# Adding the causal mask on VectorE while it takes the maximum, and turning one more pair with VectorE's block transpose

## The chip, the cores and the metric

The kernel runs on one core of a Trainium2 chip. The metric is the device time of one execution in microseconds (us), given as the median of the runs. A change of about 0.5% (4.4 us here) is what can be told from no change.

## The reference

Three layers follow each other, for a batch of 4 sequences of 448 positions with 768 channels. All data are 32-bit floats.

```python
q_n, k_n = rmsnorm(q, g_q), rmsnorm(k, g_k)          # (4, 12 heads, 448, 64)
x = softmax(q_n @ k_n.T / 8) @ v                     # attention; heads side by side: (4, 448, 768)
u = x + token_mlp(x)                                 # relu MLP along the 448 positions, 256 hidden
y = u + relu(u @ w_ch1) @ w_ch2                      # MLP along the channels, 1536 hidden
# four experts, each a single causal head of width 64; the two best by gate are mixed
for e in range(4):
    s = (y @ wq[e]) @ (y @ wk[e]).T / 8
    s = where(causal, -1e9, s)                       # position i sees positions up to i
    a = softmax(s)                                   # s - max, exp, divide by the sum
    out += gate[:, :, e] * (a @ (y @ wv[e]) @ wo[e])
```

## The kernel before

**Pairs.** Heads are worked on two at a time. A sequence has 6 plain pairs of the first attention, named (b, pr) with pr from 0 to 5, and 2 causal pairs (four experts). The 448 positions lie in 4 chunks of 112 partitions (`CP`). Each pair goes through `stack` (loads q and k, scales k), `score` and `finish` (the product with v).

**Scores and softmax** (`weighted`). For a chunk c, TensorE writes the scores of both heads into one PSUM tile, 112 partitions by 2 heads by w columns (L596). w is 448 for a plain pair and 112 times (c + 1) for a causal one. Two chunks make one step of TensorE work. For a causal pair the step ends with one more matmul per chunk and head (L601): the identity `eye` times `veil`, a 112x112 tile that holds -1e9 above its diagonal, is accumulated into the last 112 columns. VectorE then takes the negated maxima of both heads in one `tensor_reduce` (`top`, L566) into `nm`, and ScalarE computes exp(score + nm) with the row sum as a second output, one instruction per head (L581).

**Transposing the weights.** The product with v needs the softmax weights transposed, and there are two ways. `flip` does it with TensorE transposes of 112-column blocks into PSUM (L626 for plain pairs, 28 of them for a pair; L650 for causal pairs), and copies out of PSUM by ScalarE or VectorE (L431, L432). `turn` does it with VectorE: 4 transposes by 32x32 blocks (L700), and then 16 copies between groups of 32 partitions (quarters) that put the blocks in their places (L712), on VectorE, ScalarE or GpSimd. With `turn` the scores lie on 128 partitions, the positions of q are read in another order (arranged on the host in `_layout`), and the row of softmax sums reaches DRAM by one DMA instead of four (`spread`). A pair that uses it is called wide. Before the change all plain pairs of the third and fourth batch are wide (`b >= LATE`, LATE = 2), 12 pairs in all.

**What else runs.** `channel` is the MLP along the channels, by far the largest part of TensorE's work; its products (`mm3`, L520) are three matmuls on a split of each number into two parts. In the first batch the weights are also unpacked and split, by ScalarE, VectorE and GpSimd (L465 to L472, `split`), and kept in DRAM for the later batches. `project` makes the experts' q, k and v, and `combine` the output.

**The order of work.** Nothing is ordered by hand. Every step is entered with `add`, with its engine or engines and an estimated cost, and `Plan` lays out all steps of all four batches with a list schedule by priority, ten rounds, of which the one with the shortest estimated span is used. Each engine then runs its instructions in that order. A changed cost or a changed step can therefore move other steps too. The plain pairs of batch b + 1 are entered together with the causal pairs of batch b - 1, around `channel(b)`, so that attention and MLP can be laid beside each other. Tiles come from rings of buffers (`RING`): score, transposed and weight tiles of all pairs share the tag "s" with 3 buffers, and there are 2 PSUM tiles of scores. `flip` takes 2 buffers of "s" for a pair, `turn` 3.

`Stats` computes the inverse norms of q and k for a group of pairs (`root`, L835 to L846, a Newton iteration on VectorE or a power on GpSimd, by the planner's costs).

Of the kernel before, what the change touches and what calls it, by code (L numbers as in the profile page):

```python
# [9 lines left out]
F32 = mybir.dt.float32  # L10
F32R = mybir.dt.float32r
# [3 lines left out]
ALU = mybir.AluOpType  # L15
# [4 lines left out]
MASKED = -1e9  # L20
# [21 lines left out]

FAST = {(0, 0), (0, 1)}

LATE = 2


class Buf:
# [268 lines left out]
def kernel(  # L317
# [15 lines left out]
    nc = tc.nc  # L333
# [3 lines left out]
    P, CP, NCH, D = 128, 112, 4, 64  # L337
    S = CP * NCH
# [53 lines left out]
    def rows_ns(n):  # L392
        return 1.652 * n

    def flip_ns(n):
# [4 lines left out]

    ident = cp.tile([P, P], F32, tag="ident", name="ident")
    make_identity(nc, ident)
    dark = cp.tile([CP, CP], F32, tag="dark", name="dark")
    nc.gpsimd.memset(dark, 0.0)
    nc.gpsimd.affine_select(
        dark, dark, [[-1, CP]], ALU.is_ge, MASKED, base=0, channel_multiplier=1)
    veil = cp.tile([CP, CP], F32R, tag="veil", name="veil")
    nc.vector.tensor_copy(veil, dark)
    eye = cp.tile([CP, CP], F32R, tag="eye", name="eye")
    nc.vector.tensor_copy(eye, ident[:CP, :CP])  # L410
    ggs = cp.tile([P, 2], F32, tag="ggs", name="ggs")
    nc.scalar.dma_start(ggs, gg)
    half = cp.tile([CP, 1], F32, tag="half", name="half")
# [138 lines left out]
    def weighted(st, causal, sm, col, rq, alone, wide=False):  # L552

        q, k = st
        R = P if wide else CP  # L560
        s = sbuf([R, NCH, 2, S], F32, "s")
        nm = sbuf([P, NCH, 2], F32, "nm")

        def top(c, pst, w):
            dve(2 * w, [pst], [(nm, c)],
                lambda e: e.tensor_reduce(  # L566
                    nm.t[:R, c], pst.t[:R, :, :w], axis=AX.X, op=ALU.max, negate=True))

        def scale(cs):
            at = slice(cs[0], cs[-1] + 1)  # L570
            add({"DVE": (130, True), "POOL": (200, True)}, 0, [rq[0]], [(nm, c) for c in cs],
                lambda e: ENG[e].tensor_tensor(  # L572
                    nm.t[:R, at], nm.t[:R, at], rq[1]()[:, :, at].rearrange("p j c -> p c j"),
                    op=ALU.mult))

        def exps(c, pst, w):
            for j in range(2):
                add("ACT", act_ns(w, True, 2 if rq is None else 3),
                    [pst, (nm, c), *([rq[0]] if rq else [])],
                    [(s, (j, c)), (sm, 4 * (col + j) + c)],  # L580
                    lambda j=j: nc.scalar.activation(  # L581
                        s.t[:, c, j, :w], pst.t[:R, j, :w], AF.Exp,
                        bias=nm.t[:R, c, j : j + 1],
                        scale=1.0 if rq is None else rq[1]()[:, j, c : c + 1],
                        accum_out=sm.t[:, col + j, c : c + 1]))

        width = [CP * (c + 1) if causal else S for c in range(NCH)]
        for cs in [(c,) for c in range(NCH)] if alone else [(0, 1), (2, 3)]:
            ps = {c: pss() for c in cs}

            def mms(ps=ps):
                for c, pst in ps.items():
                    w = width[c]
                    for j in range(2):
                        me = slice(64 * j, 64 * j + 64)
                        nc.tensor.matmul(  # L596
                            pst.t[:R, j, :w], q.t[me, CP * c : CP * c + R], k.t[me, :w],
                            start=True, stop=not causal)
                for c, pst in ps.items() if causal else ():
                    for j in range(2):  # L600
                        nc.tensor.matmul(  # L601
                            pst.t[:CP, j, width[c] - CP : width[c]], eye, veil,
                            start=False, stop=True)

            add("PE", sum(rows_ns(width[c]) + (290 if causal else 0) for c in cs),
                [q, k], list(ps.values()), mms, mode="rows")
            for c, pst in ps.items():
                top(c, pst, width[c])
            if rq is not None:
                scale(cs)  # L610
            for c, pst in ps.items():
                exps(c, pst, width[c])
        return s
# [234 lines left out]
    class Stats:  # L848


        def __init__(self, b, qs, ks):
            n, m = len(qs), len(ks)
            self.qs, self.ks = qs, ks
            R = self.R = P if b >= LATE else CP
            st = self.st = sbuf([R, 3, 64], F32, "st")
            x, y, z = (lambda k=k: st.t[:CP, k, : 8 * (n + m)] for k in range(3))
            if R > CP:
                add("POOL", pool_ns(64), [], [st], lambda: nc.gpsimd.memset(st.t[96:, 1], 1.0))
            at = lambda t, pr: 8 * (ks.index(pr) + n if t else qs.index(pr))
            self.at = at  # L860
            for pr in sorted({*qs, *ks}):
                if (b, pr) in FAST:
                    for t in (1, 0):
                        if pr not in (qs, ks)[t]:
                            continue
                        q, part, qv = natural(b, pr, t)
                        sq = pss()
                        o = at(t, pr)
                        add("ACT", act_ns(512, True), [(q, part)], [sq],
                            lambda sq=sq, qv=qv, t=t: nc.scalar.activation(  # L870
                                sq.t[:CP, 0], qv()[:, t].rearrange("p g d -> p (g d)"), AF.Square))
                        dve(512, [sq], [(st, o)], lambda e, sq=sq, o=o: e.tensor_reduce(
                            x()[:, o : o + 8], sq.t[:CP, 0].rearrange("p (g d) -> p g d", d=D),
                            axis=AX.X, op=ALU.add))
                    continue
                q, part, qv = natural(b, pr, 0)
                i = qs.index(pr)
                x0 = lambda i=i: x().rearrange("p (t i g) -> p t i g", t=2, i=n)[:, :, i]
                add({"ACT": (act_ns(1024), False), "POOL": (pool_ns(1024), True)}, 0, [], [(q, part)],
                    lambda e, qv=qv: nc.scalar.activation(qv(), qv(), AF.Square) if e == "ACT"  # L880
                    else nc.gpsimd.tensor_mul(qv(), qv(), qv()))
                add({"DVE": (dve_ns(1024), False),
                     "POOL": (sum(pool_ns(16 << k) for k in range(6)), True)}, 0,
                    [], [(q, part), (st, i)], lambda e, x0=x0, qv=qv: fold(e, x0(), qv()))
            add({"DVE": (11 * (150 + 8 * (n + m)), True), "POOL": (400 + 1330 * (n + m), True)},
                0, [], [st], lambda e: root(e, x(), y(), z()))
            if (b, ks[0]) in FAST:

                q, part, qv = natural(b, ks[0], 1)
                kd = self.kd = sbuf([CP, NCH, 2, D], F32, "xn")  # L890
                o = at(1, ks[0])
                dve(512, [st, (q, part)], [kd], lambda e: e.tensor_tensor(
                    kd.t.rearrange("p c j d -> p j c d"),
                    qv()[:, 1].rearrange("p (j c) d -> p j c d", j=2),
                    y()[:, o : o + 8].rearrange("p (j c) -> p j c", j=2).unsqueeze(3)
                    .to_broadcast([CP, 2, NCH, D]),
                    op=ALU.mult), port=True)
                return
            rs = self.rs = plan.buf(dr, [2 * m, S], F32, f"rs_{b}_{ks[0]}")
            load(20, [st], [rs], lambda: nc.sync.dma_start(  # L900
                rs.t.rearrange("g (p c) -> p g c", c=NCH),
                y()[:, 8 * n :].rearrange("p (g c) -> p g c", c=NCH)))

        def q(self, pr):
            o = self.at(0, pr)
            return self.st, lambda: self.st.t[: self.R, 1, o : o + 8].rearrange(
                "p (j c) -> p j c", j=2)

        def k(self, pr):
# [21 lines left out]
    class Pair:  # L931
# [10 lines left out]
        def stack(self):  # L942
# [1 line left out]
                self.st = ex[self.b][2][self.pr]  # L944
                return
            b, pr = self.b, self.pr
            wide = self.wide = b >= LATE
            v = self.v = sbuf([P, NCH, 2, D], F32, "v")
            q, k = sbuf([P, S + 16], F32, "q"), sbuf([P, S], F32, "k")
            load(237, [], [q], lambda: nc.sync.dma_start(q.t, qkt[b, pr, 0]))  # L950
# [277 lines left out]
def _layout(i):  # L1228
# [7 lines left out]
    for at in FAST:  # L1236
        kn[at] = chunks(x[:, 1])[at]
    qn = chunks(x[:, 0]).copy()
    qn[LATE:] = rows(x[:, 0])[LATE:]
    nat = np.stack([qn, kn], axis=3).reshape(b, h // 2, s // 4, 2, 2 * 4, d)  # L1240
    ends = [(0, 512 - s), (0, 0)]
    v = np.pad(x[:, 2], [(0, 0)] * 3 + ends)
    v[:, :, 1] = np.pad(x[:, 2, :, 1], [(0, 0)] * 2 + [ends[0][::-1], (0, 0)])
    vals = v.reshape(b, h // 2, 2, 4, 128, d).transpose(0, 1, 4, 3, 2, 5)
    qkt = x[:, :2].transpose(0, 2, 1, 3, 5, 4).reshape(b, h // 2, 2, 2 * d, s).copy()
    late = qkt[LATE:, :, 0]
    qkt[LATE:, :, 0] = (
        late.reshape(*late.shape[:-1], s // 4, 4).swapaxes(-1, -2).reshape(late.shape))
    qkt = np.pad(qkt, [(0, 0)] * 4 + [(0, 16)])
    g = np.stack([i["g_q"], i["g_k"]], axis=1)  # L1250
    gg = np.concatenate([g, g], axis=0)
# [54 lines left out]
```

## Time and profile before

| what | us |
|---|---|
| median of 3 runs (875.44 to 878.80) | 878.48 |
| the profiled execution, its own time | 877.03 |
| its span in the trace | 875.2 |
| TensorE (PE) busy in the span | 834.5 |
| VectorE (DVE) busy | 609.2 |
| ScalarE (ACT) busy | 460.9 |
| GpSimd (POOL) busy | 122.0 |

The profiled execution is 1.45 us below the median, and 1.8 us of its time lie outside the span of the trace. Busy time of TensorE is modelled: its matmuls overlap, so the mean of one matmul is longer than the distance from one to the next. Where the text needs the price of matmuls it takes the distance between starts.

### The profile page before, as it was taken

Reading aid. Unit: us, or ns where it says so; the run is one execution under the profiler, and the core shown is the slowest. Engines: PE = TensorE matmul, PEld = TensorE weight load, DVE = VectorE, ACT = ScalarE, POOL = GpSimd, SP = SyncE. Lnnn points to the kernel's source line nnn. Section 1 sums busy time; section 2 is a strip of 40 time slices with the busy share of each in tenths; the row PEclk is TensorE's granted clock in tenths of the full one; section 3 lists DMA queues with packets and bytes.
Section 4 is the critical chain, followed back from the end, with each engine's and each line's share of the span. In section 5 each row is a group of like instructions: output and inputs, shape, how many; then the busy total and the mean of one; then the engine's idle time right before and its main releaser. Section 6 shows DMA issues by size and latency. Waiting matters only on the chain.

```text
span 875.2 us, 13600 instructions
## 1 busy us (share of the span) xinstructions
PE 834.5 (95%) x4656; PEld 645.1 (74%) x4656; DVE 609.2 (70%) x1254; ACT 460.9 (53%) x1075; POOL 122.0 (14%) x154
## 2 busy tenths in 40 slices
PE   2899899999999999999999999999999999999998
PEld 1345478777768886887676786887776799998886
DVE  6988889899997568637699677846588671224342
ACT  5798756677665447324376655513286630002443
POOL 3234310011031011010131100100131100001000
PEclk9999999999999999999999999999999999999999
DMA  7656568888778926797655724696555316676334
GB/s 221 164 166 216 166 184 274 278 268 289 255 222 266 309 76 204 203 271 241 169 170 140 208 70 124 185 279 183 177 159 155 107 53 187 219 237 203 105 132 163
DMA packets 109749, 168.41 MB, mean 192 GB/s; under 512 B 17936, under 2 KB 76432, under 8 KB 109680
## 3 DMA queue, kind: packets, MB, share of 16 engines
q1 hardware_dynamic: 109536, 167.54, 63.5%
q8 instruction: 37, 0.61, 0.3%
q14 instruction: 32, 0.26, 0.1%
q10 hardware_dynamic: 144, 0.00, 0.0%
HBM read 136.66 MB, written 30.84 MB: 191 GB/s over the span
## 4 chain that ended last, share of the span: by engine, by line
PE 73%; DVE 15%; ACT 5%; DMA 4%; issue 2%; SPq 0%; DVEq 0%; ACTq 0%
PE a L520 50%; PE s L596 8%; PE m L725 8%; DVE nm L566 3%; ACT s L581 3%; PE m L751 2%; PE s L650 2%; DVE s L712 2%; DMA whl<-kept_c 2%; PE s L626 2%; DVE wraw L470 1%; DMA nat<-in_nat_dram 1%; DVE wraw L472 1%; PE s L601 1%; DVE s L700 1%
## 5 line engine op out<-in xcount | busy, mean ns | idle before, releaser
L520 PE MATMUL a<-uhl,whl 128*128 128x448 f32 x1152 | 244.4, 367 | 4.4 <-DVE hid L1097 2.6
L520 PEld LDWEIGHTS a<-uhl,whl 128*128 128x128 f32 x1152 | 214.0, 189 | 33.4 <-issue 8.7
L520 PE MATMUL a<-hid,whl 128*128 128x448 f32 x864 | 184.9, 367 | 2.5 <-DVE u L1108 1.6
L520 PEld LDWEIGHTS a<-hid,whl 128*128 128x128 f32 x864 | 159.4, 188 | 28.8 <-issue 9.3
L581 ACT ACTIVATE s<-s,nm,st 112x448 f32<-112x448 f32 (+1 forms) x192 | 137.1, 724 | 82.4 <-POOL nm L572 28.6
L566 DVE TENSOR_REDUCE nm<-s 112x2 f32<-112x896 f32 (+4 forms) x128 | 123.8, 996 | 35.8 <-PE s L601 18.7
L596 PE MATMUL s<-k,q 64*112 64x448 f32 (+4 forms) x512 | 113.2, 555 | 9.6 <-ACT s L581 8.0
L436 ACT ACTIVATE hid<-a 128x448 fp32r<-128x448 f32 x41 | 22.3, 544 | 134.1 <-PE a L520 134.0
L725 PE MATMUL m<-s,v 128*64 128x448 f32 x384 | 77.5, 546 | 0.0
L596 PEld LDWEIGHTS s<-k,q 64*112 64x112 f32 (+1 forms) x512 | 41.1, 184 | 49.2 <-issue 24.0
L1108 DVE TENSOR_TENSOR u<-a,u 128x448 f32<-128x448 f32 x72 | 44.7, 621 | 44.1 <-PE a L520 43.3
L1097 DVE SCALAR_TENSOR_TENSOR hid<-a,hid 128x448 fp32r<-128x448 f32 x48 | 29.7, 620 | 60.2 <-ACT hid L436 60.0
L712 ACT COPY s<-s 32x896 f32<-32x896 f32 (+1 forms) x74 | 61.9, 837 | 6.2 <-DVE s L700 3.9
L712 DVE COPY s<-s 32x896 f32<-32x896 f32 (+1 forms) x88 | 59.6, 677 | 1.5
L700 DVE STREAM_TRANSPOSE s<-s 128x896 f32<-128x896 f32 x48 | 51.3, 1094 | 12.3 <-ACT s L581 10.8
L450 POOL TENSOR_TENSOR uhl<-u,uhl 128x448 fp32r<-128x448 f32 x22 | 25.9, 1180 | 218.8 <-PE a L520 116.0
L725 PEld LDWEIGHTS m<-s,v 128*64 128x64 f32 x384 | 25.4, 136 | 41.5 <-issue 40.0
L431 ACT ACTIVATE s<-s 112x448 f32<-112x448 f32 (+5 forms) x76 | 36.3, 528 | 19.2 <-PE s L650 15.2
L581 ACT ACTIVATE s<-s,nm 112x112 f32<-112x112 f32 (+3 forms) x64 | 30.8, 494 | 25.8 <-DVE nm L566 25.6
L465 ACT ACTIVATE wraw<-w 128x256 f32<-128x256 f32 (+3 forms) x72 | 33.3, 465 | 13.5 <-DMA w<-in_wc_dram 11.3
L520 PE MATMUL a<-whl,uhl 128*112 128x260 f32 x288 | 39.1, 288 | 0.0
L581 ACT ACTIVATION_READ_ACCUMULATOR s<-s,nm,st 112x1 f32 (+1 forms) x192 | 38.9, 203 | 0.0
(146 smaller groups left out, 1047.2 us busy)
## 6 DMA issues: line engine op xcount, KB each, us to landing
whl<-kept_c SPq DMA_DIRECT2D x72, 384.0 KB
whl<-kept_c SPq DMA_DIRECT2D x108, 256.0 KB
w<-in_wc_dram SPq DMA_DIRECT2D x24, 384.0 KB
kept_c<-whl SPq DMA_DIRECT2D x24, 384.0 KB
w<-in_wc_dram SPq DMA_DIRECT2D x36, 256.0 KB
kept_c<-whl SPq DMA_DIRECT2D x36, 256.0 KB
whl<-kept_qk SPq DMA_DIRECT2D x24, 384.0 KB
nat<-in_nat_dram SPq DMA_DIRECT2D x19, 448.0 KB
```

Of the source, the lines that this page charges most:

```text
L431: lambda e: nc.scalar.activation(dst(), src(), AF.Copy) if e == "ACT"
L450: either(n, reads, writes, lambda e: e.tensor_tensor(dst()[:, 1], src(), f(dst()[:, 0]), op=ALU.subtract))
L465: add("ACT", act_ns(n), [(d, 1)], [(r, part)], lambda: nc.scalar.activation(rf(), half(1).bitcast(F32), AF.Copy, scale=2.0 ** -112))
L520: nc.tensor.matmul(acc, lhs[:, x], rhs[:, y], start=first and i == 0, stop=last and i == 2)
L566: lambda e: e.tensor_reduce(nm.t[:R, c], pst.t[:R, :, :w], axis=AX.X, op=ALU.max, negate=True))
L581: lambda j=j: nc.scalar.activation(s.t[:, c, j, :w], pst.t[:R, j, :w], AF.Exp, bias=nm.t[:R, c, j : j + 1], scale=1.0 if rq is None else r ...
L596: nc.tensor.matmul(pst.t[:R, j, :w], q.t[me, CP * c : CP * c + R], k.t[me, :w], start=True, stop=not causal)
L700: dve(2 * S + 64, [(s, (j, r)) for j in range(2)], [(t, r)], lambda e, r=r: e.transpose(t.t[:, :, 32 * r : 32 * r + 32], s.t[:, r].rearran ...
L712: lambda e, a=a, o=o, w=w, at=at: (nc.scalar.copy if e == "ACT" else ENG[e].tensor_copy)(at(p.t[32 * o : 32 * o + 32, :, P * a : P * a + N ...
L725: nc.tensor.matmul(av.t[64 * j : 64 * j + 64, q0:S], vat(j, c)[1](), p.t[:, j, c, q0:] if causal else p.t[:, 3 * j + c], start=c == 0, sto ...
L1097: lambda e, hl=hl, pa=pa: e.scalar_tensor_tensor(hl.t[:, 1], pa.t[:, :S], 0.0, f(hl.t[:, 0]), op0=ALU.max, op1=ALU.subtract))
L1108: dve(S, [pa], [u], lambda e, u=u, pa=pa: e.tensor_add(u.t, pa.t[:, :S], u.t))
```

## The change

The mask is no longer accumulated by TensorE. `veil` becomes a 112x448 tile of zeros with the mask in its last 112 columns, and for a causal pair VectorE runs one `tensor_tensor_reduce` per chunk and head (`veiled`): it adds `veil` to the scores, multiplies by -1, writes that back to PSUM over the scores, and leaves the minimum, which is the negated maximum, in `nm`. ScalarE then takes exp with a scale of -1. The tiles `dark` and `eye` go.

`LATE` becomes a pair, (1, 5): the last plain pair of the second batch is wide too, so `turn` takes the place of `flip` for it. The group of inverse norms that holds it lies on 128 partitions. The planner's cost of `root` on VectorE rises from 150 to 192 ns an instruction.

```diff
-LATE = 2
+LATE = (1, 5)
...
-    dark = cp.tile([CP, CP], F32, tag="dark", name="dark")
-    nc.gpsimd.memset(dark, 0.0)
+    veil = cp.tile([CP, S], F32, tag="veil", name="veil")
+    nc.gpsimd.memset(veil, 0.0)
     nc.gpsimd.affine_select(
-        dark, dark, [[-1, CP]], ALU.is_ge, MASKED, base=0, channel_multiplier=1)
-    veil = cp.tile([CP, CP], F32R, tag="veil", name="veil")
-    nc.vector.tensor_copy(veil, dark)
-    eye = cp.tile([CP, CP], F32R, tag="eye", name="eye")
-    nc.vector.tensor_copy(eye, ident[:CP, :CP])
+        veil[:, S - CP :], veil[:, S - CP :], [[-1, CP]], ALU.is_ge, MASKED, base=0,
+        channel_multiplier=1)
...
+        def veiled(c, pst, w):
+            for j in range(2):
+                dve(w, [], [pst, (nm, (c, j))], lambda e, j=j: e.tensor_tensor_reduce(
+                    pst.t[:CP, j, :w], pst.t[:CP, j, :w], veil[:, S - w :], -1.0, 3e38,
+                    op0=ALU.add, op1=ALU.min, accum_out=nm.t[:CP, c, j : j + 1]))
...
-                    [pst, (nm, c), *([rq[0]] if rq else [])],
+                    [pst, (nm, (c, j) if causal else c), *([rq[0]] if rq else [])],
...
-                        scale=1.0 if rq is None else rq[1]()[:, j, c : c + 1],
+                        scale=-1.0 if rq is None else rq[1]()[:, j, c : c + 1],
...
-                            start=True, stop=not causal)
-                for c, pst in ps.items() if causal else ():
-                    for j in range(2):
-                        nc.tensor.matmul(
-                            pst.t[:CP, j, width[c] - CP : width[c]], eye, veil,
-                            start=False, stop=True)
-
-            add("PE", sum(rows_ns(width[c]) + (290 if causal else 0) for c in cs),
+                            start=True, stop=True)
+            add("PE", sum(rows_ns(width[c]) for c in cs),
                 [q, k], list(ps.values()), mms, mode="rows")
             for c, pst in ps.items():
-                top(c, pst, width[c])
+                (veiled if causal else top)(c, pst, width[c])
...
-            R = self.R = P if b >= LATE else CP
+            R = P if (b, max(qs + ks)) >= LATE else CP
...
-            add({"DVE": (11 * (150 + 8 * (n + m)), True), "POOL": (400 + 1330 * (n + m), True)},
+            add({"DVE": (11 * (192 + 8 * (n + m)), True), "POOL": (400 + 1330 * (n + m), True)},
...
-            wide = self.wide = b >= LATE
+            wide = self.wide = (b, pr) >= LATE
```

The other edits follow from these two: `Stats.q` and the host's `_layout` ask for the pair (b, pr) instead of the batch.

## Rows read from the trace of the kernel before

**Rows 1.** The page's first part: busy us, share of the span, instructions.

```profile
PE 834.5 (95%) x4656; PEld 645.1 (74%) x4656; DVE 609.2 (70%) x1254; ACT 460.9 (53%) x1075; POOL 122.0 (14%) x154
```

**Rows 2.** Busy time by stretch: PE, PEld, DVE, ACT, POOL, PEclk, DMA share, GB/s.

```profile
240.00:270.00 30.00, 29.55 (x159) 20.04 (x155) 29.28 (x58) 18.81 (x46) 11.39 (x10) 1.00 0.76 245
270.00:300.00 30.00, 30.00 (x212) 25.10 (x211) 17.02 (x45) 15.52 (x44) 1.20 (x2) 1.00 0.90 269
300.00:330.00 30.00, 30.00 (x224) 24.62 (x223) 20.46 (x65) 14.47 (x43) 2.75 (x3) 1.00 0.37 130
330.00:360.00 30.00, 27.32 (x122) 20.85 (x121) 27.21 (x44) 21.35 (x42) 4.23 (x5) 0.94 0.71 215
...
420.00:450.00 30.00, 30.00 (x149) 20.91 (x147) 22.45 (x35) 15.91 (x34) 4.86 (x6) 1.00 0.53 150
...
840.00:860.00 20.00, 20.00 (x151) 16.63 (x151) 10.63 (x48) 9.24 (x25) 0.00 (x0) 1.00 0.40 141
```

**Rows 3.** The mask's matmuls: a step on TensorE's timeline (start, us).

```profile
276.97 0.60 PE L601 MATMUL s<-veil,eye 112*112 112x112 f32 x4
277.41 2.64 PE L520 MATMUL a<-uhl,whl 128*128 128x448 f32 x12
```

**Rows 4.** All instructions of line 601: ns min/median/max, first and last start.

```profile
L601 PE MATMUL s<-veil,eye x64: 260/262/308, 277.0 to 841.9; 112*112 112x112 f32 x64
```

**Rows 5.** Timeline of TensorE: transposes of the second batch's last pair.

```profile
271.40 1.87 PE L626 MATMUL s<-ident,s 112*128 112x112 f32 x16
273.04 0.86 PE L520 MATMUL a<-uhl,whl 128*128 128x448 f32 x3
273.74 1.32 PE L626 MATMUL s<-ident,s 112*128 112x112 f32 x12
274.82 1.46 PE L520 MATMUL a<-uhl,whl 128*128 128x448 f32 x6
```

**Rows 6.** Groups by shape, VectorE and ScalarE: busy us, mean ns | idle before.

```profile
L566 DVE TENSOR_REDUCE nm<-s 112x2 f32<-112x896 f32 x56 | 60.1, 1085 | 19.1 <-PE s L601 11.6 <-PE s L596 7.3
...
L1097 DVE SCALAR_TENSOR_TENSOR hid<-a,hid 128x448 fp32r<-128x448 f32 x48 | 29.7, 620 | 60.2 <-ACT hid L436 60.0
...
L1061 DVE SCALAR_TENSOR_TENSOR h<-a,h 128x256 fp32r<-128x256 f32 x24 | 9.9, 421 | 11.5 <-ACT h L436 11.2
...
L566 DVE TENSOR_REDUCE nm<-s 112x2 f32<-112x672 f32 x8 | 6.8, 848 | 0.0
...
L566 DVE TENSOR_REDUCE nm<-s 112x2 f32<-112x448 f32 x8 | 4.9, 616 | 0.0
...
L566 DVE TENSOR_REDUCE nm<-s 112x2 f32<-112x224 f32 x8 | 3.1, 389 | 7.2 <-PE s L601 7.1
...
L581 ACT ACTIVATION_READ_ACCUMULATOR s<-s,nm 112x1 f32 x64 | 13.1, 204 | 0.0
```

**Rows 7.** Timeline of the last causal step: its last exponential, the first transposes.

```profile
845.05 0.54 ACT L581 ACTIVATE s<-s,nm 112x336 f32<-112x336 f32 x1
...
847.59 0.83 PE L650 MATMUL s<-ident,s 112*112 112x112 f32 x7
```

**Rows 8.** Groups by line: the 12 turns (48 transposes, 192 copies).

```profile
L712 ACT COPY s<-s 32x896 f32<-32x896 f32 (+1 forms) x74 | 61.9, 837 | 6.2 <-DVE s L700 3.9 <-DVE inv L672 1.3
L712 DVE COPY s<-s 32x896 f32<-32x896 f32 (+1 forms) x88 | 59.6, 677 | 1.5
L700 DVE STREAM_TRANSPOSE s<-s 128x896 f32<-128x896 f32 x48 | 51.3, 1094 | 12.3 <-ACT s L581 10.8 <-ACT s L712 1.2
...
L712 POOL COPY s<-s 32x896 f32<-32x896 f32 (+1 forms) x30 | 26.7, 890 | 57.6 <-DVE s L700 29.8 <-DVE inv L672 26.6
```

**Rows 9.** Timeline of the start, VectorE: the first `root` and two casts.

```profile
5.00 0.69 DVE L872 TENSOR_REDUCE st<-s 112x8 f32<-112x512 f32 x1 [0.92 <-ACT s L870]
...
7.94 0.69 DVE L892 TENSOR_TENSOR xn<-nat,st 112x512 f32<-112x512 f32 x1
8.55 0.21 DVE L408 CAST veil<-dark 112x112 fp32r<-112x112 f32 x1
8.68 0.21 DVE L410 CAST eye<-ident 112x112 fp32r<-112x112 f32 x1
```

More of the change, by code (lines that the diff above doesn't have):

```diff
@@ L852, in __init__ @@
             n, m = len(qs), len(ks)
-            self.qs, self.ks = qs, ks
-            R = self.R = P if b >= LATE else CP
+            self.b, self.qs, self.ks = b, qs, ks
+            R = P if (b, max(qs + ks)) >= LATE else CP
             st = self.st = sbuf([R, 3, 64], F32, "st")
@@ L905, in q @@
             o = self.at(0, pr)
-            return self.st, lambda: self.st.t[: self.R, 1, o : o + 8].rearrange(
+            R = P if (self.b, pr) >= LATE else CP
+            return self.st, lambda: self.st.t[:R, 1, o : o + 8].rearrange(
                 "p (j c) -> p j c", j=2)
@@ L1238, in _layout @@
     qn = chunks(x[:, 0]).copy()
-    qn[LATE:] = rows(x[:, 0])[LATE:]
+    late = [(i, j) for i in range(b) for j in range(h // 2) if (i, j) >= LATE]
+    for at in late:
+        qn[at] = rows(x[:, 0])[at]
     nat = np.stack([qn, kn], axis=3).reshape(b, h // 2, s // 4, 2, 2 * 4, d)
@@ L1245, in _layout @@
     qkt = x[:, :2].transpose(0, 2, 1, 3, 5, 4).reshape(b, h // 2, 2, 2 * d, s).copy()
-    late = qkt[LATE:, :, 0]
-    qkt[LATE:, :, 0] = (
-        late.reshape(*late.shape[:-1], s // 4, 4).swapaxes(-1, -2).reshape(late.shape))
+    for at in late:
+        qkt[at][0] = qkt[at][0].reshape(-1, s // 4, 4).swapaxes(-1, -2).reshape(-1, s)
     qkt = np.pad(qkt, [(0, 0)] * 4 + [(0, 16)])
```

## The prediction

> **What bounds the kernel now.** I read the page's first part, then the busy time by stretch, then the timelines of the places that the change touches. TensorE is busy for 834.5 of 875.2 us [rows 1]; the reader is to see that no other engine comes near. The stretches say it more sharply: in those that hold causal pairs (270 to 330, 840 to 860) TensorE is busy for the whole stretch, while VectorE has 13.0 of 30, 9.5 of 30 and 9.4 of 20 us free [rows 2]. There, TensorE's instructions in order set the time, and one that goes makes everything behind it earlier by its distance to the next. Two stretches are different. From 240 to 270 VectorE is busy 29.28 of 30 us with the weights of the first batch, and from 330 to 360 TensorE has gaps (27.32 of 30) beside a full VectorE (27.21) [rows 2]. What is saved or added there need not pass on.
>
> **The mask leaves TensorE.** A causal pair has two steps, each with 2 chunks of 2 heads, so 4 mask matmuls; 8 pairs make 16 steps and 64 matmuls, which is the count in the trace [rows 4]. Their mean duration counts overlap, so I take starts: the four begin at 276.97 and the next product at 277.41, which is 0.44 us [rows 3]. The other 15 steps look alike, at 0.43 or 0.44. The sum is 16 x 0.44 = 7.0 us, all in stretches in which TensorE has no gap. The switch from score matmuls, which use 64 rows of the array, to full ones stays: it falls to the next product instead of the mask.
>
> **The mask arrives on VectorE.** Before, one reduction serves both heads: 389, 616, 848 and 1085 ns for the four widths of a pair [rows 6], 2.94 us together. The trace holds no fused add-and-minimum. The nearest rows have the same sources, one in PSUM and one in SBUF: 421 ns for 256 columns and 620 ns for 448 [rows 6], so 1.04 ns a column and 155 ns to begin; the reduction of 896 columns fits the same law (155 + 932 = 1087). By that law the new instructions take 271, 388, 504 and 621 ns, twice each: 3.57 us, 0.63 more a pair. A gain is excluded: the same columns are read, at the rate that all these rows have, with twice the beginnings. Delivering the minimum may cost extra; ScalarE's exponentials have a row of their own for the row sum, 204 ns [rows 6]. With 0.2 us each, a pair takes 3.57 + 1.6 = 5.2 us, 2.2 more. The upper bound is half the rate, as an operation that writes PSUM and keeps a running minimum might have: 2 x (4 x 0.155 + 1120 x 0.00208) = 5.9, with the reads 7.5 us, 4.6 more a pair, 37 us over all eight. I take 2.2 (18 us over all), because it is put together from the nearest rows. The Trainium skill says so too, in "VectorE: DVE Perf Modes", section "Two Vector instructions with no wait between them": on VectorE an operation that also writes out its accumulator is two instructions. By that rule the sum is 2.2 a pair, without it 0.63; no run here shows it for VectorE.
>
> None of this costs time as long as VectorE has room (two pairs need 4.4 us where it has some 22 free, 270 to 330 [rows 2]) and the exponentials still come before the transposes that wait for them. In a pair's second step the maxima took 0.85 + 1.09 = 1.9 us and will take 2 x (0.50 + 0.62) + 0.8 = 3.1, so 1.1 later. In the last pair the last exponential ends at 845.6 and the transposes begin at 847.59 [rows 7]: 2.0 us of room, filled with products. The 1.1 fit, partly also since the first head's exponential need no longer wait for the second's maximum. What is queued on VectorE behind these instructions are copies and normalisations of project, which lie in the same gaps. I cost the mask on VectorE at nothing, and keep 8 x (4.6 - 2.0) = 21 us for the upper bound.
>
> **The turned pair.** TensorE loses 28 transposes of pair (1, 5): 273.04 - 271.40 and 274.82 - 273.74 make 2.7 us [rows 5], again without gaps. Four copies out of PSUM go. There come 4 block transposes at 1.09 us and 16 copies; by the 12 turns of the trace, a turn takes 51.3 / 12 = 4.3 us of transposes and (59.6 + 61.9 + 26.7) / 12 = 12.4 us of copies, of which VectorE does 5.0, ScalarE 5.2 and GpSimd 2.2 [rows 8]. VectorE thus gets 9.3 us. Its cover is the stretch from 270 to 300, right behind the scores of this pair, where VectorE has 13.0 us free, ScalarE 14.5 and GpSimd nearly all [rows 2]; turns in the third and fourth batch show that this can be done with TensorE full (420 to 450: 30.00 busy [rows 2]). Both additions fit there, since one causal pair needs 2.2. If they don't fit, the next late thing is the product with v of this pair, and through the 3 buffers of "s" the exponentials of the first causal pair.
>
> The Trainium skill speaks against this edit: the rules for kernel authors in "VectorE: DVE Perf Modes" give 128x128 transposes to TensorE where the target may be PSUM. The rows agree on the effort, 16.7 us of three engines for 2.7 of TensorE; by the rule the edit loses, by the stretch it gains, since TensorE alone is full.
>
> The rest is small. SP issues one DMA instead of four for the row of sums, VectorE one transpose less; the score matmuls keep their columns. At the start two casts of 0.21 us leave VectorE [rows 9], and GpSimd fills a wider tile; nothing waits for that one before the first causal pair. The dearer `root` can send the first group (11 x 200 = 2200 against 1730 on GpSimd; before 1738) to GpSimd. On VectorE it ran from 5.69 to 7.94, 2.25 us [rows 9]; GpSimd needs two operations, which I can't price, so I keep 2 us either way and take nothing.
>
> **The sum.** The profiled execution's own time is 877.0; 877.0 - 7.0 - 2.7 = 867.3. It lies 1.45 under the median of the runs shown, so the median should be 878.5 - 9.7 = 868.8, rounded to 869, 1.1% faster.
>
> **The rivals.**
>
> *The gain before 330 is lost in the next stretch.* Some 4 steps (1.8 us) and the turned pair (2.7) lie before 330. Behind them VectorE is full and TensorE has gaps [rows 2], so TensorE may just arrive earlier and wait longer. That costs 4.5: 878.5 - 5.2 = 873.3. Against it speaks that VectorE's work ahead of 330 has slack too and can come earlier.
>
> *The turn meets the full VectorE.* If the planner lays pair (1, 5) earlier, its 9.3 us on VectorE fall into the stretch up to 270 with 0.7 us free [rows 2], the split weights of the MLP come later, and TensorE waits for them: 878.5 - 9.7 + 9.3 = 878, no change. Against it: the pair is the last of its batch and is transposed only from 271.40 on [rows 5]. The Trainium skill's rule on transposes, named above, would give this time.
>
> *The fused operation is slow (the slower side).* At half rate every causal pair's maxima take 4.6 us longer, 2.0 of it covered; TensorE, in order, waits at the transposes of each pair: +21 - 9.7, so 890. It decides from 3.2 us longer a pair, where 8 x 1.2 eats the gain. Against it: a two-source row with PSUM runs at full rate [rows 6].
>
> **How the numbers follow.** The forecast has 0.60, with a range of its own from 865 to 873 (2 us for `root`, some for the new order). The first rival has 0.14, the second 0.15, the slow operation 0.11. The first rival's 873.3 lies just within the 0.5% (4.4 us, about what a measurement can tell) below 878.5, so I count two thirds of it as faster: faster 0.69, same 0.20, slower 0.11. The range from 865 to 880 takes in the first two rivals and leaves out the slow operation and a little below.
>
> **What would show it.** Right: no matmul of line 601's kind and no gap of TensorE in its place; the new instructions at 0.27 to 0.62 us, perhaps with a read beside each; 168 + 140 transposes of plain pairs; TensorE still full in causal stretches, its busy sum lower, and a turn between 270 and 300. Wrong: the fused rows near 1 us for 448 columns; TensorE waiting for exponentials or copies before the causal transposes; gaps of TensorE before 290 that end with split weights; or 330 to 360 with larger gaps by what was saved.

## The result and the profile after

The median went from 878.14 us (4 runs with those of the comparison) to 864.09 (863.90 to 865.67, 4 runs), a ratio of 0.9849 with a 95% interval from 0.982 to 0.9879. That is 14.05 us faster, where 9.5 were forecast, and 0.9 us below the range from 865 to 880. In us the interval reaches from 10.6 to 15.8, so the 9.5 are outside it, but not by much.

The page of the changed kernel, first part, answers to [rows 1]:

```profile
span 862.3 us, 13533 instructions
PE 823.4 (95%) x4564; PEld 636.1 (74%) x4564; DVE 619.5 (72%) x1341; ACT 468.0 (54%) x1077; POOL 149.8 (17%) x167
```

TensorE has 92 matmuls fewer, the 64 of the mask and the 28 transposes. VectorE gained only 10.3 us, less than the 18 + 9.3 that the forecast gave it, and GpSimd 27.8, which nothing in the forecast accounts for: work was handed over to it elsewhere, in an order laid anew.

The changed kernel's timeline of TensorE at the first causal step answers to [rows 3], and its groups by shape on VectorE to [rows 6]:

```profile
269.48 0.83 PE L599 MATMUL s<-k,q 64*112 64x112 f32 x8
270.25 4.47 PE L517 MATMUL a<-uhl,whl 128*128 128x448 f32 x21
```

```profile
L563 DVE CUSTOM_DVE_ANT_0 s<-s,veil 112x448 f32<-112x448 f32 x16 | 10.2, 637 | 4.8 <-PE s L599 4.4
...
L563 DVE DVE_READ_ACCUMULATOR2_ANT nm<- 112x1 f32 x64 | 8.8, 138 | 0.0
L563 DVE CUSTOM_DVE_ANT_0 s<-s,veil 112x336 f32<-112x336 f32 x16 | 8.5, 534 | 0.1
...
L563 DVE CUSTOM_DVE_ANT_0 s<-s,veil 112x224 f32<-112x224 f32 x16 | 6.7, 418 | 0.1
...
L563 DVE CUSTOM_DVE_ANT_0 s<-s,veil 112x112 f32<-112x112 f32 x16 | 4.7, 292 | 1.6 <-PE s L599 1.6
```

The product now follows the scores directly. The fused instruction runs at full rate (292 ns for 112 columns, 637 for 448: 1.03 ns a column), and each has a read of the accumulator of its own.

The turned pair, on the changed kernel's timelines of VectorE and TensorE (in brackets idle time before, and what ended it):

```profile
260.26 2.09 DVE L697 STREAM_TRANSPOSE s<-s 128x896 f32<-128x896 f32 x2
...
268.05 2.10 DVE L697 STREAM_TRANSPOSE s<-s 128x896 f32<-128x896 f32 x2
...
277.22 2.65 DVE L709 COPY s<-s 32x896 f32<-32x896 f32 x3
```

```profile
276.60 2.42 PE L517 MATMUL a<-whl,uhl 128*112 128x260 f32 x18 [0.38 <-DVE q L545]
280.13 3.23 PE L722 MATMUL m<-s,v 128*64 128x448 f32 x16 [1.10 <-DVE s L709]
```

The turn spreads over 20 us. Its first four microseconds on VectorE fall into the stretch up to 270, which VectorE fills (28.88 of 30 us busy, below). The product with v waits 1.10 us for the turn's last copies, and the 0.38 us before 276.60 is a wait for an instruction of VectorE that stands between these copies.

The surprise stands further ahead. In the kernel before, TensorE's timeline at the first product of the channel MLP, long before the first causal step, and at the first product with the 260-wide weights of `project`:

```profile
124.47 2.88 PE L520 MATMUL a<-uhl,whl 128*128 128x448 f32 x13 [1.29 <-DVE u L1079]
...
286.19 4.58 PE L520 MATMUL a<-whl,uhl 128*112 128x260 f32 x36
```

The first of them in the changed kernel (the second stands above, at 276.60):

```profile
117.35 4.96 PE L517 MATMUL a<-uhl,whl 128*128 128x448 f32 x24
```

The changed kernel leads by 7.1 us at the first, where it has left out nothing yet, and by 9.6 at the second, where it has left out two mask steps and the 28 transposes, 3.6 us. So most of the lead at these places was won where the change takes nothing away from TensorE. It is time in which TensorE waited. Stretch from 0 to 90 (columns as in [rows 2]) and the longest wait of TensorE in the whole run, kernel before and then changed kernel:

```profile
0.00:90.00 90.00, 64.62 (x348) 33.79 (x348) 75.27 (x157) 69.10 (x169) 32.08 (x54) 1.00 0.64 187
PE m L751 <- DVE xn L892: 16.1, 2, 8.8
```

```profile
0.00:90.00 90.00, 71.73 (x380) 36.78 (x382) 74.28 (x154) 74.01 (x180) 37.02 (x53) 1.00 0.67 191
PE m L748 <- DVE xn L889: 8.9, 1, 8.9
```

TensorE is busy 7.1 us longer in these 90 us, and of two long waits for VectorE's normalised k (`xn`) one is gone. But this lead is not kept. Over the whole span the gaps of TensorE are 875.2 - 834.5 = 40.7 us before [rows 1] and 862.3 - 823.4 = 38.9 after, 1.8 less; so some 5 us of it are waited away further on. The span is 12.9 us shorter: 11.1 less busy time, of which 9.7 is the sum of the forecast, and 1.8 less waiting. The other 1.4 us of busy time may be the granted clock, which was 0.94 from 330 to 360 in the kernel before [rows 2] and 1.00 in the changed one; that it was this is not shown. The stretches of the changed kernel, answering to [rows 2]:

```profile
240.00:270.00 30.00, 27.64 (x152) 19.87 (x151) 28.88 (x60) 18.04 (x44) 7.94 (x6) 1.00 0.78 246
270.00:300.00 30.00, 28.52 (x203) 23.02 (x200) 24.37 (x77) 18.98 (x53) 6.58 (x7) 1.00 0.92 265
300.00:330.00 30.00, 28.37 (x192) 22.85 (x190) 24.26 (x56) 15.39 (x38) 5.04 (x5) 1.00 0.27 91
330.00:360.00 30.00, 27.54 (x134) 23.24 (x133) 21.05 (x38) 13.75 (x24) 4.63 (x4) 1.00 0.83 255
```

From 240 to 330 TensorE is no longer full: it has 5.5 us of gaps where it had 0.5 [rows 2]. Besides the 0.38 and 1.10 us above they are these (timeline of TensorE):

```profile
244.85 2.47 PE L517 MATMUL a<-hid,whl 128*128 128x448 f32 x11 [1.55 <-POOL whl L447]
249.91 0.67 PE L517 MATMUL a<-hid,whl 128*128 128x448 f32 x2 [0.81 <-DVE whl L447]
309.33 2.07 PE L517 MATMUL a<-t,h 128*128 128x448 f32 x9 [1.63 <-DVE h L1059]
```

The first two end with split weights (`whl`), which the prediction had named as a sign of being wrong. They lie ahead of the pair's first transposes at 260.26, so it is not the turn that made these weights late.

At the start the first group's root went to GpSimd, as the forecast allowed. Changed kernel, timeline, against [rows 9]:

```profile
5.29 0.26 POOL L834 TENSOR_SCALAR st<-st 112x8 f32<-112x8 f32 x1 [3.21 <-DVE st L869]
...
5.62 1.67 POOL L836 TENSOR_TENSOR st<-st,half 112x8 f32<-112x8 f32 x1
...
8.13 0.68 DVE L889 TENSOR_TENSOR xn<-nat,st 112x512 f32<-112x512 f32 x1
```

It takes 2.0 us there (5.29 to 7.29), against 2.25.

### The profile page after: what moved, and what is told of

Read it like the earlier page. It is cut to its first block, busy times and chain, and to the rows that moved or that the text cites. A ratio compares the mean times of both kernels' runs of the same rounds, so it can differ in the third digit from the quotient of the medians.

```text
span 862.3 us, 13533 instructions
## 1 busy us (share of the span) xinstructions
PE 823.4 (95%) x4564; PEld 636.1 (74%) x4564; DVE 619.5 (72%) x1341; ACT 468.0 (54%) x1077; POOL 149.8 (17%) x167
## 4 chain that ended last, share of the span: by engine, by line
PE 73%; DVE 14%; DMA 5%; ACT 5%; issue 2%; SPq 0%; POOL 0%; ACTq 0%; DVEq 0%
PE a L517 52%; PE s L599 8%; PE m L722 8%; DVE nm L569 3%; ACT s L584 2%; PE m L748 2%; DMA w<-in_wc_dram 1%; DMA nat<-in_nat_dram 1%; PE s L647 1%; DVE wraw L467 1%; ACT s L428 1%; DVE s L709 1%; PE s L623 1%; DVE s L697 1%; DMA whl<-kept_c 1%
## 5 line engine op out<-in xcount | busy, mean ns | idle before, releaser
L517 PE MATMUL a<-hid,whl 128*128 128x448 f32 x864 | 187.0, 368 | 3.6 <-POOL whl L447 1.5
L584 ACT ACTIVATE s<-s,nm,st 128x448 f32<-128x448 f32 (+1 forms) x192 | 137.0, 724 | 65.1 <-DVE nm L575 41.8
L569 DVE TENSOR_REDUCE nm<-s 128x2 f32<-128x896 f32 (+1 forms) x96 | 101.7, 1082 | 10.4 <-PE s L599 10.1
L709 ACT COPY s<-s 32x896 f32<-32x896 f32 (+1 forms) x92 | 76.2, 829 | 9.8 <-DVE s L697 7.3
L697 DVE STREAM_TRANSPOSE s<-s 128x896 f32<-128x896 f32 x52 | 55.6, 1094 | 14.1 <-ACT s L584 11.5
L709 POOL COPY s<-s 32x896 f32<-32x896 f32 (+1 forms) x29 | 25.6, 882 | 94.6 <-DVE inv L669 53.5
L428 ACT ACTIVATE s<-s 112x448 f32<-112x448 f32 (+5 forms) x65 | 32.2, 539 | 16.2 <-PE s L647 11.2
```

Source lines behind the costliest of these rows:

```text
L428: lambda e: nc.scalar.activation(dst(), src(), AF.Copy) if e == "ACT"
L517: nc.tensor.matmul(acc, lhs[:, x], rhs[:, y], start=first and i == 0, stop=last and i == 2)
L569: lambda e: e.tensor_reduce(nm.t[:R, c], pst.t[:R, :, :w], axis=AX.X, op=ALU.max, negate=True))
L584: lambda j=j: nc.scalar.activation(s.t[:, c, j, :w], pst.t[:R, j, :w], AF.Exp, bias=nm.t[:R, c, j : j + 1], scale=-1.0 if rq is None else ...
L697: dve(2 * S + 64, [(s, (j, r)) for j in range(2)], [(t, r)], lambda e, r=r: e.transpose(t.t[:, :, 32 * r : 32 * r + 32], s.t[:, r].rearran ...
L709: lambda e, a=a, o=o, w=w, at=at: (nc.scalar.copy if e == "ACT" else ENG[e].tensor_copy)(at(p.t[32 * o : 32 * o + 32, :, P * a : P * a + N ...
```

## The experiments

Each ratio compares a kernel with the kernel before in the same session. The kernel before had medians from 878.14 to 881.04 in these sessions, so ratios are compared here, and not medians.

**The three parts, alone and in pairs.** The price of root, the mask and the turned pair are independent edits of the text, so the kernel can be built with any of them. The theory after the result (S) was that the price moves the start; the rivals were that mask and turn gave everything (M), and that each new order is a draw (N). By order is meant all that the planner lays out, so also which engine a step goes to.

The price alone, on the kernel before:

```diff
-            add({"DVE": (11 * (150 + 8 * (n + m)), True), ...
+            add({"DVE": (11 * (192 + 8 * (n + m)), True), ...
```

> The kernel before with one edit: the planner's price of root on VectorE is 192 ns an instruction instead of 150. Theory S (the start): the dearer price sends the first group's root to GpSimd and with it rearranges the first 30 us, which is where the changed kernel is ahead by 7 us at the first product of the channel MLP; this edit alone then gives that lead (6 to 8 us at that product) and keeps 4 to 8 of it at the end: 870 to 874. Rival M (the mask and the turn): the lead of the start would be eaten by the stretches with gaps of TensorE behind it, and the two named edits give all of the 14 us; then this kernel ends at 876 to 880.

Measured: 874.56, ratio 0.9942 [0.9912, 0.9973].

The changed kernel with the price put back (192 to 150 in the same line):

> The changed kernel with the price of root put back to 150. Theory S: the start is that of the kernel before (first product of the channel MLP near 124 us), and the mask and the turn give the 9.7 us of the forecast: 867 to 871. Rival M: 862 to 866, as the changed kernel. Rival N (every new order is a draw of some us, and the parts do not add up): anywhere from 862 to 875.

Measured: 866.85, ratio 0.9873 [0.9832, 0.9914].

The mask alone: the changed kernel with

```diff
-LATE = (1, 5)
+LATE = (2, 0)
...
-            add({"DVE": (11 * (192 + 8 * (n + m)), True), ...
+            add({"DVE": (11 * (150 + 8 * (n + m)), True), ...
```

> The kernel before with the mask on VectorE alone (price of root 150, the second batch's last pair turned by TensorE). By the forecast's term it gives 7.0 us: 870 to 872. Theory S agrees with that; rival M wants more than 7, so 866 or less; if the fused instructions were in the way it would be 875 or more.

Measured: 875.43, ratio 0.9951 [0.9925, 0.9978], less than the term.

The turned pair alone: the kernel before with the change's edits of this part.

```diff
-LATE = 2
+LATE = (1, 5)
...
-            wide = self.wide = b >= LATE
+            wide = self.wide = (b, pr) >= LATE
```

> The kernel before with the second batch's last pair turned by VectorE alone (price of root 150, the mask on TensorE). By the forecast's term it gives 2.7 us: 875 to 876. Rival M: 872 or less. If the turn meets the full VectorE: 878 or more.

Measured: 878.49, ratio 0.9986 [0.9952, 1.002]. The interval holds the term's 2.7 us (0.997) and no gain as well.

The mask and the price, from the changed kernel:

```diff
-LATE = (1, 5)
+LATE = (2, 0)
```

> The changed kernel without the turned pair (mask on VectorE, price of root 192). If the parts add as they were measured singly (mask 0.9951, root 0.9942): 0.989. If they strengthen each other as mask and turn did (0.9873 together against 0.9937 by their product): 0.986 or less.

Measured: 877.42, ratio 0.9983 [0.996, 1.0005].

The turned pair and the price, from the kernel with the turned pair alone:

```diff
-            add({"DVE": (11 * (150 + 8 * (n + m)), True), ...
+            add({"DVE": (11 * (192 + 8 * (n + m)), True), ...
```

> The kernel before with the turned pair and the price of root 192, the mask on TensorE. If the parts add (turn 0.9986, root 0.9942): 0.993. If each new order is a draw of some us: anywhere from 0.988 to 1.000.

Measured: 872.94, ratio 0.9928 [0.9901, 0.9954].

With all eight, each edit's worth in four surroundings (nothing, and one or both of the others) is, in per cent of the time: mask 0.49, 1.13 (with the turn), -0.41 (with the price), 0.80 (with both); turn 0.14, 0.78 (with the mask), 0.14 (with the price), 1.34; price 0.58, -0.32 (with the mask), 0.58 (with the turn), 0.24. The means are 0.50, 0.60 and 0.27, in us 4.4, 5.3 and 2.4, each uncertain by some 2 us. Mask and turn are worth 9.7 us on average, the forecast's sum, but that the sum fits is partly luck: the mask's mean is below its 7.0 and the turn's is above its 2.7. One surrounding gives -0.4% and another 1.1% for the same mask, more than the intervals explain. S and M both fall: the price is no fixed 5 us, and the parts don't add. S had also named a sign in the trace, the start of the first product of the channel MLP: near 117 us with the price alone, near 124 with the price put back. It is the other way round. Timelines of TensorE, the price alone and the price put back:

```profile
126.66 1.56 PE L520 MATMUL a<-uhl,whl 128*128 128x448 f32 x7
```

```profile
117.71 1.48 PE L517 MATMUL a<-uhl,whl 128*128 128x448 f32 x6 [0.57 <-DVE u L1077]
```

So the lead at the start does not come from the price, and a lead there does not decide the end: mask and price without the turn start this product at 119.46 and end at 0.9983. N stays, as the name for what is left: it says that a new order moves the time, and not by what.

**The same order, one thing swapped.** To take the new order out of the comparison, each step keeps its planned place, and only what a step issues is changed. First the changed kernel's order with the mask on TensorE again:

```diff
-                dve(w, [], [pst, (nm, (c, j))], lambda e, j=j: e.tensor_tensor_reduce(
-                    pst.t[:CP, j, :w], pst.t[:CP, j, :w], veil[:, S - w :], -1.0, 3e38,
-                    op0=ALU.add, op1=ALU.min, accum_out=nm.t[:CP, c, j : j + 1]))
+                dve(w, [], [pst, (nm, (c, j))], lambda e, j=j: j or e.tensor_reduce(
+                    nm.t[:CP, c], pst.t[:CP, :, :w], axis=AX.X, op=ALU.max, negate=True))
...
-                            start=True, stop=True)
+                            start=True, stop=not causal)
+                for c, pst in ps.items() if causal else ():
+                    for j in range(2):
+                        nc.tensor.matmul(
+                            pst.t[:CP, j, width[c] - CP : width[c]], eye, veil,
+                            start=False, stop=True)
```

> The changed kernel in its own planned order, step for step, but the causal pairs' mask is accumulated by TensorE again and one reduction takes both heads' maxima (the second of the two planned VectorE steps is empty). Nothing is planned anew. If the term of the sum holds (T: 16 x 0.44 us that nothing hides), this is 7.0 us slower than the changed kernel: about 871, a ratio of 0.992 to 0.993 to the kernel before. If the saved time is mostly taken back by gaps that stand behind the causal steps (G): 866 to 868, a ratio of 0.986 to 0.988.

Measured: 871.54 (864.77 to 873.56), ratio 0.9904 [0.9869, 0.9939], 0.55% or 4.8 us over the changed kernel's 0.9849. That lies between T and G, and the interval holds both.

Then the order of the kernel before, with the fused instructions of both heads as one step in the place of its reduction, and no mask matmuls:

> The kernel before in its own planned order, but the mask matmuls are gone and VectorE runs two fused instructions where it ran one reduction. T: 7.0 us faster than before, ratio 0.992. G: 2 to 4 us, ratio 0.9955 to 0.998.

Measured: 876.88, ratio 0.9983 [0.9961, 1.0006]: 1.5 us, a little under G's range, and T falls. Here the trace shows who takes much of the gain back. Apart from the mask both kernels run the same matmuls in the same order, so a matmul's start can be compared with itself. Kernel before, timeline of TensorE after the first batch's causal pairs:

```profile
345.20 8.49 PE L520 MATMUL a<-uhl,whl 128*128 128x448 f32 x36
354.62 7.48 PE L520 MATMUL a<-uhl,whl 128*128 128x448 f32 x36 [0.93 <-DVE hid L1097]
361.94 8.57 PE L520 MATMUL a<-hid,whl 128*128 128x448 f32 x42
370.85 2.68 PE L520 MATMUL a<-hid,whl 128*128 128x448 f32 x12 [0.34 <-DMA whl<-kept_c]
```

The same order with the mask on VectorE:

```profile
343.33 7.48 PE L517 MATMUL a<-uhl,whl 128*128 128x448 f32 x36
353.81 8.84 PE L517 MATMUL a<-uhl,whl 128*128 128x448 f32 x36 [3.00 <-DVE hid L1097]
362.49 8.93 PE L517 MATMUL a<-hid,whl 128*128 128x448 f32 x42
372.60 1.68 PE L517 MATMUL a<-hid,whl 128*128 128x448 f32 x7 [1.19 <-DMA whl<-kept_c]
```

It comes 1.87 us earlier (345.20 against 343.33), waits 3.00 instead of 0.93 us for VectorE, then 1.19 instead of 0.34 for a DMA, and is 1.75 us late at the last row. In between TensorE's clock fell, too. Stretches of this kernel (columns as in [rows 2]):

```profile
346.00:352.00 6.00, 4.81 (x25) 4.16 (x23) 5.88 (x9) 5.94 (x12) 0.73 (x2) 1.00 0.71 229
352.00:358.00 6.00, 4.19 (x14) 3.81 (x15) 5.38 (x11) 3.24 (x5) 0.00 (x0) 0.72 0.38 128
```

A granted clock of 0.72 is a mix of the two levels, 2.4 and 1.2 GHz; it follows the wait of 3 us. In the kernel before the clock fell in this place as well, a little earlier (0.83 from 340 to 346, 0.88 from 346 to 352). By these figures it cost both the same, some 1.7 us, so the difference here is the waits: 2.07 us more for VectorE and 0.85 for the DMA.

This is not the whole of it. At 483.10 the kernel before is only 0.11 us ahead; but over the 11 steps that follow the swapped kernel gains 1.29 us instead of 4.8. The rest goes in smaller waits. Among them is one of causal transposes for ScalarE's exponentials (waits of TensorE from 480 to 560; the kernel before has none of these there). It is not the fused instructions that hold them up: the first two end at 489.46, but ScalarE is busy with copies of a turn and begins its exponentials at 490.44, where the kernel before begins at 489.64:

```profile
PE s L650 <- ACT s L586: 0.7, 1, 0.7
```

**Orders as draws.** The next kernels differ from the changed one by the price of root alone, 170, 185 or 210 in the place of 192. They have the same kinds of work, and the first root is on GpSimd in all. The rival to N is that what counts of the price is this place of the first root (R); then all of them should be as fast as the changed kernel. The first of them:

```diff
-            add({"DVE": (11 * (192 + 8 * (n + m)), True), ...
+            add({"DVE": (11 * (170 + 8 * (n + m)), True), ...
```

> The changed kernel with the planner's price of root at 170 instead of 192. No instruction is added or removed, and the first root is on GpSimd as in the changed kernel; only the order differs. Theory N (the forecast's direct terms hold on average, and each new order is a draw of some us around them): somewhere between 864 and 874, not the same as the changed kernel. Theory R (what counts of the price is the first root on GpSimd): the same as the changed kernel within 1.5 us, 0.985 of the kernel before.

Measured: 867.50, ratio 0.9847 [0.9786, 0.9909], the same as the changed kernel, as R has it.

> The same with a price of 185. N: another draw, 862 to 874; the planner's own estimate is 2.9 us under the changed kernel's here, so if its estimates carry over, 861. R: 0.985 of the kernel before.

Measured: 865.41, ratio 0.9827 [0.9767, 0.9887], with R's 0.985 inside the interval.

> The same with a price of 210. N: another draw, 864 to 876; the planner's own estimate is 3.3 us over the changed kernel's. R: 0.985 of the kernel before.

Measured: 862.20, ratio 0.9778 [0.9716, 0.984], the lowest of all kernels; its interval still touches the changed kernel's. But prices 170 and 210 were run in one session, and there the runs of 210 (856.88 to 864.75) all lie below those of 170 (866.33 to 867.84), 5.3 us between the medians. So an order alone moves the changed kernel's time too. The planner's own estimate had put 210 behind the changed kernel by 3.3 us.

And the changed kernel's order with the first root on VectorE after all:

```diff
-                0, [], [st], lambda e: root(e, x(), y(), z()))
+                0, [], [st], lambda e: root("DVE" if n + m == 1 else e, x(), y(), z()))
```

> The changed kernel in its own planned order, but the first group's root runs on VectorE at the place where GpSimd's was planned, as eleven small instructions (2.25 us in the kernel before) instead of two on GpSimd. R: TensorE's first transposes come some 0.5 to 2 us later and the end by 2 to 5. N: the place itself is worth less than 1.5 us at the end, 0.985 to 0.987.

Measured: 863.84, ratio 0.9819 [0.9758, 0.9879]. Its first transposes start 1.1 us later, and nothing of that is left at the end. Timeline of TensorE:

```profile
9.98 0.98 PE L748 MATMUL m<-ident,xn 112*128 112x112 f32 x4 [9.98 <-DVE st L834]
```

against 8.87 in the changed kernel; the first product of the channel MLP starts at 116.95, 0.4 us earlier than there. In this order the place of the root is worth nothing that the trace or the time shows, and R falls here.

**Was the kernel before a poor draw?** The kernel before with the price at 170 and 210, and the first swap of the mask again, in the orders of price 170 and 210. The edits are those shown above, with 150 or 192 replaced in the line of the price:

> The kernel before with the planner's price of root at 170, nothing else. If the kernel before is a typical draw (typical): 0.995 to 1.005. If it is a poor one (poor), as the price of 192 with 0.994 hints: 0.990 to 0.995.

Measured: 874.96, ratio 0.9957 [0.9935, 0.9978], by the expectation's bounds just typical.

> The kernel before with the price at 210. Typical: 0.995 to 1.005. Poor: 0.990 to 0.995.

Measured: 872.75, ratio 0.9917 [0.9886, 0.9948], poor.

> The changed kernel in the order of price 170, with the mask accumulated by TensorE again as in the first swap. Direct term whole (T): 7.0 us over price_170, ratio 0.9927 to the kernel before. Direct term partly taken back (G): 2 to 5 us over it, 0.987 to 0.990.

Measured: 872.33, ratio 0.9932 [0.9905, 0.9959], 0.85% or 7.5 us over price 170.

> The same in the order of price 210. T: 7.0 us over price_210, ratio 0.986. G: 2 to 5 us over it, 0.980 to 0.984.

Measured: 868.71, ratio 0.991 [0.9874, 0.9945], 1.32% or 11.6 us over price 210. That is more than T's 7.0, and no sum here accounts for it; two intervals meet in it, some 6 us.

By price, the kernel without the edits and the changed one:

| price of root | mask on TensorE, pair flipped | mask on VectorE, pair turned | quotient |
|---|---|---|---|
| 150 | 1 (the kernel before) | 0.9873 | 0.9873 |
| 170 | 0.9957 | 0.9847 | 0.9890 |
| 192 | 0.9942 | 0.9849 (the changed kernel) | 0.9906 |
| 210 | 0.9917 | 0.9778 | 0.9860 |

The quotients, each uncertain by 0.4 to 0.7%, have a mean of 0.9882, that is 1.18% or 10.3 us for mask and turn. All three other prices beat 150 without the edits, by 3.8, 5.1 and 7.3 us: the kernel before had the poorest of its four orders. Two things keep this from being shown as chance. The three have the first root on GpSimd in common, and in the order of the kernel before its place was not swapped alone. And in both columns the dearer price goes with the shorter time nearly throughout; against a rule speaks mask and price without the turn (0.9983), slower than the mask alone (0.9951).

In the order of price 170 the swap can be followed in the trace. Timeline of TensorE, mask on TensorE, the products behind the second and the last mask step:

```profile
276.32 0.56 PE L520 MATMUL a<-whl,uhl 128*112 128x260 f32 x3
...
837.66 1.53 PE L520 MATMUL a<-whl,uhl 128*112 128x260 f32 x11
```

The same matmuls with the mask on VectorE:

```profile
277.19 0.61 PE L517 MATMUL a<-whl,uhl 128*112 128x260 f32 x3
...
832.25 1.94 PE L517 MATMUL a<-whl,uhl 128*112 128x260 f32 x14
```

From one to the other it is 561.34 us with the mask matmuls and 555.06 without, 6.28 less; 14 steps lie between, 14 x 0.44 = 6.2. So the term seems to pass on whole here. The same two products in the traces of all four swaps (start of the one, start of the other, us between them):

| order of | mask on TensorE | mask on VectorE | less |
|---|---|---|---|
| the kernel before | 281.92, 841.97: 560.05 | 280.12, 840.80: 560.68 | -0.63 |
| the changed kernel | 273.79, 831.11: 557.32 | 276.60, 830.38: 553.78 | 3.54 |
| price 170 | 276.32, 837.66: 561.34 | 277.19, 832.25: 555.06 | 6.28 |
| price 210 | 276.87, 833.65: 556.78 | 275.91, 829.14: 553.23 | 3.55 |

In each of them TensorE gains its 0.44 us at each of these steps. What waits behind the steps then differs from order to order: nothing on balance at 170, 2.7 us in two orders, and more than all of it in the order of the kernel before. (At 210 some 1.7 of the 3.55 us may be the clock, 0.72 from 334 to 340 with the mask on TensorE and 1.00 without.) One trace each is little: at the first product of the channel MLP, ahead of all that was swapped, the two traces in the changed kernel's order already stand 3.1 us apart (114.25 and 117.35).

## Why the prediction was wrong

*TensorE sets the time.* Right as far as each step goes: at each of the 14 steps followed, what stands behind it comes 0.44 us earlier, in all four orders. But a matmul that goes counts at the end only where nothing behind it is late: in the order of the kernel before, 1.5 us were left of 7.0.

*The mask's 7.0 us.* The times agree with it in orders laid with the mask on VectorE: 4.8, 7.5 and 11.6 us in three of them, a mean of 8.0, but each is uncertain by 4 to 6 us, since two intervals meet. The traces show 3.5, 6.3 and 3.5 of 6.2 between the second and the last step. So the term is right as what TensorE is spared at each step; what of it reaches the end differs from order to order.

*The fused instruction.* At full rate, as the nearest rows said, and the slow-operation rival falls. The read of the accumulator exists, as the Trainium skill's section "Two Vector instructions with no wait between them" ("VectorE: DVE Perf Modes") has it. Its price was too high: with 138 ns a read, which partly overlaps the next instruction, the last pair's two steps run from 825.94 to 827.25 and from 830.50 to 832.98 in the changed kernel, 3.8 us where the forecast had 5.2. Among the changed kernel's waits of TensorE is none of causal transposes for an exponential, so it cost nothing there, as forecast; in the order of the kernel before there is one of 0.7 us, behind copies on ScalarE.

*The turned pair.* 2.7 us by its term; 0.14 to 1.34% by surroundings, a mean of 5.3 us that holds the new orders too. It stretched over 20 us and made TensorE wait 1.1. The rules for kernel authors in the Trainium skill's "VectorE: DVE Perf Modes", which give such transposes to TensorE, did not decide: in no surrounding was the turn slower, though alone its 0.14% is no clear gain. The rival of the full VectorE came true in its condition only, and in part: the first transposes were laid into the full stretch up to 270. Its price did not come, since the gaps from 240 to 330 grew by 5.0 us and not by 9.3, and none of them ends with weights that the turn had made late.

*The gain before 330.* Its mechanism is real: in the order of the kernel before, a lead of 1.97 us (306.50 against 304.53) became a delay of 1.75 at 372. It did not decide the changed kernel, whose order differs.

*The step that failed* is the price of root: "so I keep 2 us either way and take nothing", and with it the range "2 us for `root`, some for the new order". I priced the instruction that moves, and that was right (nothing of it is left at the end in the fixed order). What the price does is to lay every step anew, and the sum took for granted that all else stays in its place. A new order can be worth more than the 4 us that the range allowed on either side: 3.8 to 7.3 us on the kernel before by the price alone, 5.3 us between two orders of the changed one. Of the measured 1.51% the price has 0.58 (5.1 us) if it is changed first (0.9942), and 0.24 (2.1 us) if it is changed last (0.9873 to 0.9849); mask and turn have the rest, 8.2 or 11.2 us. So no one split is the true one. The forecast of 9.7 us is near the mean over orders (9.7 and 10.3), and the measured pair lay above it, as it might have lain below. Why one order is good and another poor stays open. The changed kernel's lead of 7.1 us at the start is one wait of the start that is gone, but with the price put back that wait is there again (15.9 us in two waits for `xn`) and the lead too (117.71), and most of such a lead is waited away later.

## What to carry to other kernels

Where a planner lays out the program, a change of a few microseconds is measured through a new order that is worth as much: compare several orders with and without the change (a price moved a little is enough), or keep the order and swap only what a step issues. In this case a sum of removed work came near the average over orders, while its parts did not; a range for one measured pair must hold the spread of orders on both sides, here some 5 us. And work taken from the full engine pays only if the next late thing, a vector result or a DMA, comes earlier too.

## What the runs showed of the hardware

VectorE's fused add-and-minimum with one source in PSUM, writing back to PSUM, runs at 1.03 ns a column with 177 ns to begin (292 and 637 ns for 112 and 448 columns), and its accumulator comes by a second instruction of 138 ns. GpSimd's power on 8 columns took 1.67 us, as long as eight small VectorE instructions (11 in 2.25 us [rows 9]). A mask step of four 112-column matmuls took 0.44 us from start to start on TensorE, and its removal gave just that at each of the 14 steps followed, in all four orders. But a lead can be lost whole: one of 1.87 us met a wait for VectorE that grew from 0.93 to 3.00 us and one for a DMA that grew from 0.34 to 1.19, and 1.75 us were missing behind them. The granted clock fell for both kernels there, to 0.72 over 6 us in the one and to 0.83 and 0.88 over 12 us in the other.
